# Where the first token block of layer 2 is split, and which of three prologue steps goes first, in a fused attention + two-layer kernel

## The chip, the cores and the metric

One Trainium2 chip, one of its cores. The metric is the device time of one execution in microseconds; the kernel before takes 858.0 us in the median of three runs (857.73 to 858.41).

## The reference

```
x = windowed_attention(q, k, v)                 # 4 batches, 8 heads, 576 positions, 64 per head
x = x.transpose(0, 2, 1, 3).reshape(2304, 512)
x = (sigmoid(x @ w_gate) * (x @ w_val)) @ w_out # layer 1: 512 -> 1536 -> 512
h = x @ w_in                                    # layer 2: 512 -> 2048
g = maximum(h, 0) + alpha * minimum(h, 0)
return g @ w_out2                               # 2048 -> 512
```

Heads 0 to 3 look at a plain window of 32 positions, heads 4 to 7 at a window with dilation 4. All tensors are fp32.

## The kernel before, in words

Every fp32 operand is split into two fp16 halves, high and low, and a product is three passes (high by high, high by low, low by high). ScalarE makes the high half (`activation` with a scale), VectorE or GpSimd the low one (the operand less its high half).

Layer 1 goes batch by batch, b = 0 to 3, 576 tokens each. Attention of the next batch runs between its steps, so that the last batch, b = 3, has none. For each of 12 column tiles m: the gate products (`gv_mm` "g", L584), the halves of the tile before (`gv_halves(m - 1)`: L612 on ScalarE, L170 on GpSimd in the last batch and on VectorE in the others), the sigmoid (L597, ScalarE), the value products ("v", L584), and the multiply (`gv_multiply`, L602, VectorE). The tile `gt` (the halves) feeds the output products: four chunks d of 128 columns, each a sum over the 12 tiles m (`o1_mm`, L636). A chunk leaves PSUM by L654 (ScalarE), L196 takes its bound, and L656 stores it to `y_dram`. Gate, value and output products take three pairs of PSUM banks in turn: chunk (3, 0) takes the pair that value tile 10 had, which L602 of m = 10 sets free.

Layer 2 works on token blocks: block 0 (DIRECT) holds the first 256 tokens, all of batch 0, blocks 1 to 4 hold 512 each. A block's y is read back from `y_dram` (`y_load`, L870 for block 0), sums are made on GpSimd (`y_sums`, L902 for block 0), and the high and low halves `yh` by `y_high` (L925, ScalarE) and `y_low` (L929, VectorE). The products with `w_in` are L968. Block 0 has four short units of two halves with 24 matmuls each; `last_output(d, m)`, which is called ahead of each `o1_mm` of the last batch, puts one of these eight halves into the output loop at 12 (d - 2) + m = 1, 4, 6, 9, 11, 14, 16 and 19. Blocks 1 to 4 have long units of seven products of 12 matmuls (`unit`, whose first product and its copy `c1`, L1023, are `unit_begin`). Between them stand the products with `w_out2` (L1213). What the activation leaves is split by L1050 (ScalarE) and L1054 (VectorE); the last four splits of a short unit are kept in a list and done in the next one (`sums_high`, `sums_low`).

The weights of layer 2 are prepared during layer 1 in small steps (`prepare`): sums on GpSimd (L813 to L816), high halves on ScalarE (L823), low halves on VectorE (L828), stores to `w2_dram` (L840). They come back as `w_i` (L761) and, for `w_out2`, as `plain` (a first pair of tiles, `w2_ring(True)`) and `w` (three more), L1196. SyncE's queue issues all of these DMAs in the program's order. Tiles of a few tags share slots: "sg" and "gf" (two each), "xh" (two, 4608 fp16 wide), "y" (eight). The order of all engines is the order in which the program is written.

Of the kernel before, what the change touches and what calls it, by code (L numbers as in the profile page):

```python
# [8 lines left out]
F32 = mybir.dt.float32  # L9
# [15 lines left out]
def attention_moe_kernel(  # L25
# [23 lines left out]
    P = 128  # L49
# [599 lines left out]
    def o1_y(b, d):  # L649
        i = KD * b + d  # L650
        if b == 0:
            y_scale(b, d, d + 1)
        dst = tp.tile([P, S], F32, tag="sg", name="y")
        nc.scalar.activation(halves(dst), open_.pop(("o", b, d)), AF.Copy, scale=oy[:, i:i + 1])  # L654
        bound(am_y[:, i:i + 1], dst)
        nc.sync.dma_start(out=y_dram[:, d, S * b:S * b + S], in_=dst)  # L656
# [208 lines left out]
    def y_load(j):  # L865

        t0, n = blocks[j]
        for d in range(2):
            t = y[j, d] = yp.tile([P, 2, TB], F32, tag="y", name="y")
            nc.sync.dma_start(out=t[:, :, :n], in_=y_dram[:, d::2, t0:t0 + n])  # L870

    def y_places():
        t = wp.tile([P, 8192], F16, tag="w_gv2", name="yh")
        u = [xp.tile([P, 4608], F16, tag="xh", name="yh") for _ in range(2)]
        shape = dict(d=2, i=7)
        even = [t[:, 3584 * z:3584 * z + 3584].rearrange("p (d i t) -> p d i t", **shape) for z in range(2)]
        odd = [u[z][:, :3584].rearrange("p (d i t) -> p d i t", **shape) for z in range(2)]
        yh.update({j: (even, odd)[j % 2] for j in range(NJ)})
        a = w2p.tile([P, 2, TB], F32, name="temp_w", tag="temp_w")
        free = [a[:, 0], a[:, 1], t[:, 7168:].bitcast(F32)] + [x_[:, 3584:].bitcast(F32) for x_ in u]  # L880
        temps.update(zip(("a11 0", "a12", "s1", "s2", "c1"), free))

    def y_parts(j, d):
# [12 lines left out]
    def y_sums(j, d):  # L896
        n = blocks[j][1]
        t = y[j, d]
        s = y[j, d, "sums"] = yp.tile([P, 4, TB // 2], F32, tag="y", name="ys")
        add = nc.gpsimd.tensor_tensor  # L900
        if j == DIRECT:
            add(out=s[:, 0, :n], in0=t[:, 1, :n], in1=t[:, 0, :n], op=ALU.subtract)  # L902
            return
        b11, b12, b21, b22 = (t[:, i, n // 2 * h:n // 2 * h + n // 2] for i in range(2) for h in range(2))
        add(out=s[:, 0], in0=b12, in1=b11, op=ALU.subtract)
        add(out=s[:, 1], in0=b22, in1=s[:, 0], op=ALU.subtract)
        add(out=s[:, 2], in0=b22, in1=b12, op=ALU.subtract)
        add(out=s[:, 3], in0=b21, in1=s[:, 1], op=ALU.subtract)
# [14 lines left out]
    def y_high(j, d):  # L923
        for w, src in y_parts(j, d):
            nc.scalar.activation(w[0], src, AF.Copy, scale=s_y[:, j:j + 1])  # L925
# [386 lines left out]
    with tc.manual_schedule():  # L1312
# [32 lines left out]
        def do(table, k, b):  # L1345
            if k in table and not (b == 1 and k < DONE):
                table[k]()
# [80 lines left out]

        def last_output(d, m):

            if d < 2 and m == 0:
                y_load(d)
            if (d, m) == (1, 0):
                y_places()
                short_places()
            if d == 1 and m == 2:
                y_sums(0, 0)
                y_sums(0, 1)
            if d == 1 and m in (6, 8):
                y_high(0, m // 8)  # L1440
                y_low(0, m // 8)
            if d == 2 and m == 2:
                y_sums(1, 0)
                y_sums(1, 1)
            if d == 2 and m in (6, 8):
                y_high(1, m // 8)
                y_low(1, m // 8)
            if (d, m) == (2, 0):
                i = 2 * turn["m"]
                short_order.extend([6, 7, i, i + 1])  # L1450
            if (d, m) == (2, 6):
                total_scale(0)
            if (d, m) == (3, 0):
                assert not steps, len(steps)
                w2_ring(True)
                w2_fetch(fetched.popleft())
            if d > 1 and M1 * (d - 2) + m in (1, 4, 6, 9, 11, 14, 16, 19):
                k = short_units.popleft()
                if k not in running:
                    running[k] = unit_short(DIRECT, k)  # L1460
                next(running[k])
                if not short_units or short_units[0] != k:
                    in2_release()
                    while ring_i:
                        in2_fetch(coming.popleft())


        for b in range(1, B):
            late = b == B - 1
            before, after = ({}, {}) if late else attention(b + 1)  # L1470
            if late:
                coming = deque(list(range(U)) * NJ)
                short_units = deque(n for k in range(U // 2) for n in (k, k))
                running = {}
                att.close()
                w2p = ctx.enter_context(tc.tile_pool(name="w2p", bufs=1))
            m0 = EARLY if b == 1 else 0
            for m in range(m0, M1):
                gv_mm(b, m, "g")
                if m > m0:  # L1480
                    gv_halves(b, m - 1, late)
                gv_sigmoid(b, m)
                prepare(3)
                gv_mm(b, m, "v")
                gv_multiply(b, m)
                do(before, m, b)
                do(after, m, b)
                prepare(3 - (0 if late else ATTENTION.get(m, 0)), sums=False)
                if late and m in (5, 7, 9, 11):
                    in2_fetch(coming.popleft())  # L1490
                if late and m == 3:
                    for j in range(3):
                        y_sum(j)
                    for j in range(3):
                        y_power(j)
            gv_halves(b, M1 - 1, late)
            y_scale(b, 0, KD)
            for d in range(KD):
                if d == 0 and b + 1 < B:
                    x_gate_scale(b + 1, 0, M1)  # L1500
                do(before, M1 + d, b)
                for m in range(M1):
                    if m == (6 if d == 2 else 0):
                        do(after, M1 + d, b)
                    if m in (2, 6, 10):
                        prepare(5 - (0 if late or m > 2 else ATTENTION.get(M1 + d, 0)))
                    if late:
                        last_output(d, m)
                    o1_mm(b, d, m, M1)
                o1_y(b, d)  # L1510

        assert not short_units
        sums_high()
        sums_low(4)
        second_places()
        short_order.clear()
        turn["h"] = 0
# [24 lines left out]
            slots[0] -= 1  # L1542

        w2_fetch_all()
        for j in range(1, NJ):
            slots[0] = 7 * (U // 2)
            for k in range(U // 2):
# [144 lines left out]
```

## Time and profile before

| | |
|---|---|
| runs | 858.41, 858.0, 857.73 us |
| profiled execution | 857.94 us, of which the span is 856.1 us |
| mean granted TensorE clock | 0.986 |
| PE busy | 826.2 us, 97% of the span |
| DVE, ACT, POOL busy | 601.8, 438.4, 263.8 us |
| instructions | 21080 |

PE is TensorE's matmuls, PEld its weight loads beside them, DVE is VectorE, ACT is ScalarE, POOL is GpSimd, SP is SyncE, which issues the DMAs. A group of matmuls in the timeline has its start, its duration and, in brackets, the time that the engine had stood idle before it and what ended this. Ends of matmuls are modelled, so a group is best measured from its start to the next one's.

### The profile page before, as it was taken

The page shows a single profiled execution, that of the slowest core. Times are in us where ns is not written, and L with a number is a line of the kernel's source. Part 1 is how long each engine was busy: PE and PEld are TensorE (multiplying, and loading weights), DVE is VectorE, ACT ScalarE, POOL GpSimd, SP SyncE. Part 2 cuts the span into 40 slices and gives each one's busy share as a digit, 9 for nine tenths or more (in the row PEclk, how much of TensorE's full clock was granted, in tenths as well). Part 3 has the DMA queues.
Part 4 walks back from the last instruction along what each step waited for, and adds up shares of the span by engine and source line. Part 5 has one row for each costly group of instructions (what it writes and reads, how often), then busy time and mean ns, then how long its engine had stood idle before and what let it go on. Part 6 is the DMA issues. An engine that isn't in the chain of part 4 may idle for free.

```text
span 856.1 us, 21080 instructions
## 1 busy us (share of the span) xinstructions
PE 826.2 (97%) x8994; PEld 686.5 (80%) x8994; DVE 601.8 (70%) x1046; ACT 438.4 (51%) x725; POOL 263.8 (31%) x253
## 2 busy tenths in 40 slices
PE   7699999999999999999999899998999999999998
PEld 4677787877877778777887678887888888888887
DVE  5889976776687677777859767588577577566641
ACT  4767664357435453444336556465555555454420
POOL 1324252234011011020238744343442245232220
PEclk9699999999999999999999999999999999999999
DMA  9954526334454252068667867955955655675372
GB/s 319 348 184 141 191 73 218 112 121 161 149 190 154 76 202 70 1 201 251 232 218 240 286 242 284 337 204 201 340 206 202 245 183 202 239 284 198 123 230 78
DMA packets 86621, 169.86 MB, mean 198 GB/s; under 512 B 5504, under 2 KB 57856, under 8 KB 86528
## 3 DMA queue, kind: packets, MB, share of 16 engines
q1 hardware_dynamic: 86528, 168.52, 56.8%
q8 instruction: 70, 1.15, 0.6%
q14 instruction: 23, 0.19, 0.1%
HBM read 138.72 MB, written 29.79 MB: 197 GB/s over the span
## 4 chain that ended last, share of the span: by engine, by line
PE 72%; DVE 12%; DMA 9%; ACT 3%; issue 2%; SPq 2%; POOL 0%; ACTq 0%; DVEq 0%
PE banks L584 20%; PE banks L1213 18%; PE banks L968 17%; PE banks L636 13%; DMA w_dram<-halves 2%; DVE plain L189 2%; DMA plain_dram<-plain 2%; DVE plain L185 2%; PE banks L317 2%; PE banks L431 1%; DVE halves L828 1%; DMA vc<-vk 1%; DMA q<-qbd 1%; DVE plain L181 1%; DVE gf L602 1%
## 5 line engine op out<-in xcount | busy, mean ns | idle before, releaser
L584 PE MATMUL banks<-xh,w_gv 128*128 128x288 f16 x2304 | 290.6, 287 | 0.5 <-ACT sg L597 0.3
L584 PEld LDWEIGHTS <-w_gv 128*128 128x128 f16 x2304 | 223.3, 98 | 58.4 <-issue 0.9
L968 PE MATMUL banks<-yh,w_i 128*128 128x256 f16 x1536 | 189.1, 274 | 10.0 <-ACT yh L925 2.5
L968 PEld LDWEIGHTS <-w_i 128*128 128x128 f16 x1536 | 150.6, 98 | 30.3 <-issue 8.0
L636 PE MATMUL banks<-gt,w_o 128*128 128x288 f16 x1152 | 144.5, 286 | 0.9 <-POOL gt L170 0.9
L636 PEld LDWEIGHTS <-w_o 128*128 128x128 f16 x1152 | 111.8, 98 | 28.9 <-issue 1.1
L1213 PEld LDWEIGHTS <-g_gv 128*128 128x128 f16 x780 | 76.3, 98 | 8.8
L1213 PE MATMUL banks<-w,g_gv 128*128 128x256 f16 x612 | 75.5, 273 | 0.0
L1006 ACT ACTIVATE neg<-banks 128x512 f32<-128x512 f32 x72 | 42.8, 594 | 56.9 <-DVE banks L1026 40.3
L1064 POOL TENSOR_TENSOR yh<-temp_y 128x512 f32<-128x512 f32 x16 | 26.5, 1659 | 125.6 <-DVE temp_y L1014 120.8
L166 POOL TENSOR_SCALAR sc<-sc 128x1 f32<-128x1 f32 x35 | 11.7, 334 | 173.0 <-DVE sc L162 172.9
L1213 PEld LDWEIGHTS <-g_g 128*128 128x128 f16 x564 | 55.2, 98 | 6.4
L602 DVE SCALAR_TENSOR_TENSOR gf<-banks,sg 128x576 f32<-128x576 f32 x48 | 36.0, 752 | 34.4 <-PE banks L584 25.5
L597 ACT ACTIVATE sg<-banks,sc 128x576 f32<-128x576 f32 x48 | 35.3, 734 | 39.9 <-PE banks L584 30.1
L196 ACT ACTIVATE junk<-plain 128x1024 bf16<-128x1024 f32 x32 | 33.8, 1057 | 36.0 <-DVE plain L200 18.8
L170 POOL TENSOR_TENSOR gt<-gf,gt 128x576 f16<-128x576 f32 x19 | 27.7, 1457 | 75.4 <-ACT gt L612 75.2
L612 ACT ACTIVATE gt<-gf 128x576 f16<-128x576 f32 x48 | 32.4, 677 | 33.3 <-DVE gf L602 29.4
L189 DVE SCALAR_TENSOR_TENSOR plain<-words,plain 128x512 uint32<-128x512 uint32 x64 | 47.7, 765 | 1.2
L1213 PE MATMUL banks<-w,g_g 128*128 128x256 f16 x396 | 48.3, 273 | 0.0
L1054 DVE SCALAR_TENSOR_TENSOR g_gv<-temp_w,sc,g_gv 128x256 f16<-128x256 f32 (+1 forms) x37 | 26.0, 711 | 28.4 <-ACT g_gv L1050 28.4
L1023 ACT ACTIVATE temp_y<-banks 128x512 f32<-128x512 f32 x32 | 19.0, 595 | 50.9 <-PE banks L968 50.7
L185 DVE SCALAR_TENSOR_TENSOR plain<-words,plain 128x512 uint32<-128x512 uint32 x64 | 43.8, 704 | 1.2
(178 smaller groups left out, 1212.3 us busy)
## 6 DMA issues: line engine op xcount, KB each, us to landing
w_i<-wi_dram SPq DMA_DIRECT2D x40, 896.0 KB, 6.3
w<-w_dram SPq DMA_DIRECT2D x52, 512.0 KB, 8.7
words<-w_out SPq DMA_DIRECT2D x28, 512.0 KB, 5.5
plain<-w_dram SPq DMA_DIRECT2D x18, 512.0 KB, 9.5
words<-w_in SPq DMA_DIRECT2D x16, 512.0 KB, 5.2
w_dram<-halves SPq DMA_DIRECT2D x28, 256.0 KB, 5.1
q<-qbd SPq DMA_DIRECT2D x6, 1152.0 KB, 7.6
words<-w_gate SPq DMA_DIRECT2D x12, 512.0 KB, 5.3
```

What stands on the lines that cost most here:

```text
L170: engine.tensor_tensor(out=lo, in0=src, in1=hi, op=ALU.subtract)
L185: nc.vector.scalar_tensor_tensor(out=d, in0=hi, scalar=0xC0000000, in1=d, op0=ALU.bitwise_and, op1=ALU.bitwise_or)
L189: nc.vector.scalar_tensor_tensor(out=d, in0=lo, scalar=29, in1=d, op0=ALU.logical_shift_right, op1=ALU.bitwise_or)
L196: nc.scalar.activation(junk[:, :src.shape[1]], src, AF.Square, accum_out=dst)
L584: nc.tensor.matmul(ps[:, h, :], lhsT=a, rhs=x_[:, H2 * h:H2 * h + H2], start=(kk == 0 and i == 0), stop=(kk == KD - 1 and i == 2),)
L597: nc.scalar.activation(halves(sg), ps, AF.Sigmoid, scale=sgx[b][:, m:m + 1])
L602: nc.vector.scalar_tensor_tensor(out=halves(gf), in0=ps, scalar=2.0 ** -15, in1=halves(sg), op0=ALU.mult, op1=ALU.mult)
L612: nc.scalar.activation(t[:, 0, :], gf, AF.Copy)
L636: nc.tensor.matmul(ps[:, h, :], lhsT=a, rhs=x_[:, H2 * h:H2 * h + H2], start=(m == 0 and z == 0), stop=(m == M1 - 1 and z == 2),)
L968: nc.tensor.matmul(o, lhsT=h, rhs=l, start=(new and v == 0 and q == 1), stop=(q == total_), skip_group_check=True,)
L1006: nc.scalar.activation(t[:, :2 * n], src[:, :2 * n], AF.Relu, scale=-1.0)
L1213: nc.tensor.matmul(ps[:, H4 * t:H4 * t + H4].rearrange("p (c f) -> p c f", c=2), lhsT=a, rhs=x_, start=(first and k == 0 and t == 0 and z ...
```

## The change

Five edits, no arithmetic among them:

1. Block 0's y goes into one "y" tile; its load moves from the start of the last batch's output loop to the end of m = 4 of its gate and value loop. `y_sums` moves to the end of m = 6, and `y_high` and `y_low` from (d, m) = (1, 6) and (1, 8) to the ends of m = 7 and m = 8. The halves lie in an "xh" slot that `y_first` takes ahead of time, and so do the sums; even and odd blocks change places.
2. `gv_halves` of the last tile, m = 11, stands right behind its multiply, in batches 1 to 3, with its low half on VectorE.
3. In the last batch L654 writes to a "gf" slot, not an "sg" slot.
4. The first fetch of `w_out2` moves from (3, 0) to (3, 8) of the output loop.
5. The first product of the first long unit and its copy stand ahead of the last short unit's four late splits.

```diff
@@ o1_y
-        dst = tp.tile([P, S], F32, tag="sg", name="y")
+        dst = tp.tile([P, S], F32, tag="gf" if b == B - 1 else "sg", name="y")
@@ y_load
+        if j == DIRECT:
+            t = yp.tile([P, 2, 2, n], F32, tag="y", name="y")
+            for d in range(2):
+                y[j, d] = t[:, d]
+                nc.sync.dma_start(out=t[:, d], in_=y_dram[:, d::2, t0:t0 + n])
+            return
@@
+    def y_first():
+        n = blocks[DIRECT][1]
+        t = spans[0] = xp.tile([P, 4608], F16, tag="xh", name="yh")
+        z = 6 * n
+        yh[DIRECT] = [t[:, z * i:z * i + z].rearrange("p (d i t) -> p d i t", d=2, i=3) for i in range(2)]
+        temps["s2"] = t[:, 3584:].bitcast(F32)
@@ y_places
-        u = [xp.tile([P, 4608], F16, tag="xh", name="yh") for _ in range(2)]
+        u = [spans[0], xp.tile([P, 4608], F16, tag="xh", name="yh")]
...
@@ y_sums
         if j == DIRECT:
-            add(out=s[:, 0, :n], in0=t[:, 1, :n], in1=t[:, 0, :n], op=ALU.subtract)
+            s = y[j, d, "sums"] = temps["s2"][:, n * d:n * d + n].unsqueeze(1)
+            add(out=s[:, 0], in0=t[:, 1], in1=t[:, 0], op=ALU.subtract)
             return
@@ last_output
-            if d < 2 and m == 0:
-                y_load(d)
+            if (d, m) == (1, 0):
+                y_load(1)
...
-            if d == 1 and m == 2:
-                y_sums(0, 0)
-                y_sums(0, 1)
-            if d == 1 and m in (6, 8):
-                y_high(0, m // 8)
-                y_low(0, m // 8)
...
             if (d, m) == (3, 0):
                 assert not steps, len(steps)
+            if (d, m) == (3, 8):
                 w2_ring(True)
                 w2_fetch(fetched.popleft())
@@ the loop over m, behind gv_multiply(b, m)
+                if m == M1 - 1:
+                    gv_halves(b, m, False)
...
+                if late and m == 4:
+                    y_first()
+                    y_load(DIRECT)
+                if late and m == 6:
+                    y_sums(DIRECT, 0)
+                    y_sums(DIRECT, 1)
+                if late and m in (7, 8):
+                    y_high(DIRECT, m - 7)
+                    y_low(DIRECT, m - 7)
-            gv_halves(b, M1 - 1, late)
@@ behind the output loop
-        sums_high()
-        sums_low(4)
         second_places()
...
         w2_fetch_all()
+        unit_begin(1, 0, [w_i[0], w_i[1]])
+        sums_high()
+        sums_low(4)
```

TensorE's order is the same before and after. VectorE, in the last batch, from the multiply of m = 8 to that of m = 9; before (lines are those of each program: L929 before is L946 after):

```order
L602 SCALAR_TENSOR_TENSOR gf<-banks,sg 128x576
L828 SCALAR_TENSOR_TENSOR halves<-quarter,sc,halves 128x512
L828 SCALAR_TENSOR_TENSOR halves<-plain,sc,halves 128x512 x2
L828 SCALAR_TENSOR_TENSOR halves<-quarter,sc,halves 128x512
L828 SCALAR_TENSOR_TENSOR halves<-plain,sc,halves 128x512
L602 SCALAR_TENSOR_TENSOR gf<-banks,sg 128x576
```

and after:

```order
L602 SCALAR_TENSOR_TENSOR gf<-banks,sg 128x576
L828 SCALAR_TENSOR_TENSOR halves<-quarter,sc,halves 128x512
L828 SCALAR_TENSOR_TENSOR halves<-plain,sc,halves 128x512
L946 SCALAR_TENSOR_TENSOR yh<-y,sc,yh 128x512
L946 SCALAR_TENSOR_TENSOR yh<-yh,sc 128x256
L828 SCALAR_TENSOR_TENSOR halves<-plain,sc,halves 128x512
L828 SCALAR_TENSOR_TENSOR halves<-quarter,sc,halves 128x512
L828 SCALAR_TENSOR_TENSOR halves<-plain,sc,halves 128x512
L602 SCALAR_TENSOR_TENSOR gf<-banks,sg 128x576
```

The second pair of low halves of block 0 has come into this row of weight splits; the first pair stands one tile earlier, and all four are gone from behind the row of L828, where they stood ahead of the first L1014.

ScalarE, from the last output chunk into the first long unit; before:

```order
L654 ACTIVATE y<-banks,sc 128x576
L196 ACTIVATE junk,sc<-y 128x576
L1050 ACTIVATE g_gv<-yh,sc 128x256
L1050 ACTIVATE g_gv<-temp_w,sc 128x256
L1050 ACTIVATE g_gv<-yh,sc 128x256
L1050 ACTIVATE g_gv<-temp_w,sc 128x256
L1023 ACTIVATE yh<-banks 128x512
L1023 ACTIVATE temp_y<-banks 128x512
```

and after (L1040 is L1023 of before, L1067 is L1050):

```order
L654 ACTIVATE y<-banks,sc 128x576
L196 ACTIVATE junk,sc<-y 128x576
L1040 ACTIVATE yh<-banks 128x512
L1067 ACTIVATE g_gv<-yh,sc 128x256
L1067 ACTIVATE g_gv<-temp_w,sc 128x256
L1067 ACTIVATE g_gv<-yh,sc 128x256
L1067 ACTIVATE g_gv<-temp_w,sc 128x256
L1040 ACTIVATE temp_y<-banks 128x512
```

The copy `c1` has passed the four late splits.

SyncE's queue between the stores of output chunks 2 and 3; before:

```order
L656 DMA y_dram<-y 128x576
L1196 DMA plain<-w_dram 128x2048 x2
L761 DMA w_i_6622<-wi_dram 128x3584
L761 DMA w_i_6623<-wi_dram 128x3584
L761 DMA w_i_6624<-wi_dram 128x3584
L761 DMA w_i_6625<-wi_dram 128x3584
L656 DMA y_dram<-y 128x576
L1196 DMA w_7813<-w_dram 128x2048 x6
```

and after (L1213 is L1196 of before):

```order
L656 DMA y_dram<-y 128x576
L761 DMA w_i_6626<-wi_dram 128x3584
L761 DMA w_i_6627<-wi_dram 128x3584
L761 DMA w_i_6628<-wi_dram 128x3584
L761 DMA w_i_6629<-wi_dram 128x3584
L1213 DMA plain<-w_dram 128x2048 x2
L656 DMA y_dram<-y 128x576
L1213 DMA w_7802<-w_dram 128x2048 x6
```

The two `plain` fetches have moved behind the four `w_i` fetches.

## Rows read from the trace of the kernel before

**Rows 1.** Page, part 1 (busy us, share, instructions) and the DMA totals.
```profile
PE 826.2 (97%) x8994; PEld 686.5 (80%) x8994; DVE 601.8 (70%) x1046; ACT 438.4 (51%) x725; POOL 263.8 (31%) x253
...
DMA packets 86621, 169.86 MB, mean 198 GB/s; under 512 B 5504, under 2 KB 57856, under 8 KB 86528
```

**Rows 2.** Waits of PE, whole span: us in all, count, longest.
```profile
PE banks L968 <- DMA w_i<-wi_dram: 2.3, 2, 1.4
...
PE banks L968 <- ACT temp_y L1023: 1.0, 1, 1.0
```

**Rows 3.** Timeline 470 to 500: start us, us, engine, line, instruction, [idle before <-releaser].
```profile
474.82 0.67 ACT L612 ACTIVATE gt<-gf 128x576 f16<-128x576 f32 x1
...
477.20 1.72 POOL L170 TENSOR_TENSOR gt<-gf,gt 128x576 f16<-128x576 f32 x1
...
478.97 10.21 PE L636 MATMUL banks<-gt,w_o 128*128 128x288 f16 x82 [0.87 <-POOL gt L170]
...
490.97 0.71 ACT L925 ACTIVATE yh<-y,sc 128x512 f16<-128x512 f32 x1
...
491.72 0.27 PE L968 MATMUL banks<-yh,w_i 128*128 128x256 f16 x1 [2.54 <-ACT yh L925]
...
492.56 0.49 PE L968 MATMUL banks<-yh,w_i 128*128 128x256 f16 x3 [0.57 <-DVE yh L929]
...
494.09 3.86 PE L968 MATMUL banks<-yh,w_i 128*128 128x256 f16 x20 [1.04 <-DVE yh L929]
```

**Rows 4.** Windows of 1 us: us, busy of five engines, PEclk, DMA, GB/s.
```profile
494.00:495.00 1.00, 0.91 (x5) 0.66 (x5) 0.52 (x2) 0.97 (x3) 0.20 (x1) 0.50 1.04 368
```

**Rows 5.** Chain that ended last, in order of time: start us, us.
```profile
500.16 2.62 PE banks L968 x24
```

**Rows 6.** Timeline 500 to 560.
```profile
533.03 2.78 PE L968 MATMUL banks<-yh,w_i 128*128 128x256 f16 x24
...
534.66 0.19 ACT L196 ACTIVATION_READ_ACCUMULATOR junk<-y 128x1 f32 x1
534.75 0.49 ACT L1050 ACTIVATE g_gv<-yh,sc 128x256 f16<-128x256 f32 x1
...
536.34 0.57 ACT L1023 ACTIVATE yh<-banks 128x512 f32<-128x512 f32 x1
...
536.97 2.78 PE L968 MATMUL banks<-yh,w_i 128*128 128x256 f16 x24 [1.15 <-ACT yh L1023]
...
541.25 1.15 PE L1213 MATMUL banks<-plain,g_gv 128*128 128x256 f16 x9
...
546.49 0.49 PE L1213 MATMUL banks<-w,g_gv 128*128 128x256 f16 x3
```

**Rows 7.** Timeline 405 to 470.
```profile
454.39 1.71 POOL L816 TENSOR_TENSOR plain<-quarter,plain 128x512 f32<-128x512 f32 x1
...
454.90 3.44 DVE L828 SCALAR_TENSOR_TENSOR halves<-plain,sc,halves 128x512 f16<-128x512 f32 x2
...
458.27 0.74 DVE L828 SCALAR_TENSOR_TENSOR halves<-quarter,sc,halves 128x512 f16<-128x512 f32 x1
...
467.32 0.74 DVE L602 SCALAR_TENSOR_TENSOR gf<-banks,sg 128x576 f32<-128x576 f32 x1
...
469.61 0.65 PE L636 MATMUL banks<-gt,w_o 128*128 128x288 f16 x4
```

**Rows 8.** Lines, shapes apart: busy us, mean ns, idle before.
```profile
L170 DVE TENSOR_TENSOR gt<-gf,gt 128x576 f16<-128x576 f32 x29 | 23.5, 810 | 11.1 <-ACT gt L612 10.9
```

**Rows 9.** Timeline 515 to 552, SyncE's queue.
```profile
522.14 7.73 SPq L761 DMA_DIRECT2D w_i<-wi_dram  x4
...
534.47 4.82 SPq L1196 DMA_DIRECT2D w<-w_dram  x6
```

**Rows 10.** DMA issues from 521, then 547: queue, count, KB, us to landing.
```profile
plain<-w_dram SPq DMA_DIRECT2D x2, 512.0 KB, 5.7
...
plain<-w_dram SPq DMA_DIRECT2D x2, 512.0 KB, 10.1
```

More of the change, by code (lines that the diff above doesn't have):

```diff
@@ L870, in y_load @@
             nc.sync.dma_start(out=t[:, :, :n], in_=y_dram[:, d::2, t0:t0 + n])
+    spans = {}
+    def y_first():
[4 more added lines that the diff above has]
+        temps["s2"] = t[:, 3584:].bitcast(F32)
     def y_places():
         t = wp.tile([P, 8192], F16, tag="w_gv2", name="yh")
-        u = [xp.tile([P, 4608], F16, tag="xh", name="yh") for _ in range(2)]
+        u = [spans[0], xp.tile([P, 4608], F16, tag="xh", name="yh")]
         shape = dict(d=2, i=7)
-        even = [t[:, 3584 * z:3584 * z + 3584].rearrange("p (d i t) -> p d i t", **shape) for z in range(2)]
-        odd = [u[z][:, :3584].rearrange("p (d i t) -> p d i t", **shape) for z in range(2)]
-        yh.update({j: (even, odd)[j % 2] for j in range(NJ)})
+        odd = [t[:, 3584 * z:3584 * z + 3584].rearrange("p (d i t) -> p d i t", **shape) for z in range(2)]
+        even = [u[z][:, :3584].rearrange("p (d i t) -> p d i t", **shape) for z in range(2)]
+        yh.update({j: (even, odd)[j % 2] for j in range(NJ) if j != DIRECT})
         a = w2p.tile([P, 2, TB], F32, name="temp_w", tag="temp_w")
-        free = [a[:, 0], a[:, 1], t[:, 7168:].bitcast(F32)] + [x_[:, 3584:].bitcast(F32) for x_ in u]
+        free = [a[:, 0], a[:, 1], t[:, 7168:].bitcast(F32), temps["s2"], u[1][:, 3584:].bitcast(F32)]
         temps.update(zip(("a11 0", "a12", "s1", "s2", "c1"), free))
@@ L898, in y_sums @@
         t = y[j, d]
-        s = y[j, d, "sums"] = yp.tile([P, 4, TB // 2], F32, tag="y", name="ys")
         add = nc.gpsimd.tensor_tensor
         if j == DIRECT:
-            add(out=s[:, 0, :n], in0=t[:, 1, :n], in1=t[:, 0, :n], op=ALU.subtract)
+            s = y[j, d, "sums"] = temps["s2"][:, n * d:n * d + n].unsqueeze(1)
+            add(out=s[:, 0], in0=t[:, 1], in1=t[:, 0], op=ALU.subtract)
             return
+        s = y[j, d, "sums"] = yp.tile([P, 4, TB // 2], F32, tag="y", name="ys")
         b11, b12, b21, b22 = (t[:, i, n // 2 * h:n // 2 * h + n // 2] for i in range(2) for h in range(2))
```

## The prediction, made before the changed kernel ran

> **What bounds the kernel now.** The page comes first: PE is busy for 826.2 of 856.1 us [rows 1]. So the end is set by TensorE's own work and by the few places where it stands still or runs slowly; what another engine saves counts only where it ends a wait of PE. The second view is the list of PE's waits, where the question is which of them the change touches. The third is the timeline around each of these places, with the engine that released PE beside it. The fourth is the granted clock in slices of 1 us, for what a wait costs after it has ended.
>
> Read so, the last batch has three places with a wait. At 478.97 PE had stood for 0.87 us, until GpSimd had made the low half of the last `gt` tile: L612 had ended at 475.49, but L170 began only at 477.20 and took 1.72 [rows 3]. At 489.18 (478.97 + 10.21) the output products run out and the first short unit of block 0 is due, but its `yh` is not there: ScalarE begins it at 490.97, and PE stands for 2.54, 0.57 and 1.04 us in three bites, the last two until VectorE has the low halves [rows 3]. Behind these waits the granted clock is 0.50, the lower level (1.2 of 2.4 GHz) [rows 4], and the unit's 20 remaining matmuls take 3.86 us; 24 of the same kind in the stream a few us later take 2.62 [rows 3, 5]. At 536.97 PE had stood for 1.15 us until ScalarE had copied `c1` at 536.34 to 536.91, which it did only after four late splits from 534.75 on [rows 6]. The remaining waits of this size, 2.3 us for `w_i` and 1.0 us for a copy, lie in the long units, which the change does not touch [rows 2].
>
> **The change, part by part.**
>
> *Block 0's split, moved ahead (edit 1).* Removed: 2.54 + 0.57 + 1.04 = **4.15 us** of PE's wait, since the last pair of `yh` now stands among the L828 that run from 454.90 on [rows 7], some 30 us before 489.18. With the wait goes its follower: PE does not stand still, so I expect the full clock, and the 24 matmuls take 2.62 in place of 0.27 + 0.49 + 3.86 = 4.62, which is **2.00 us** more. The bounds of the second term are 0, if the clock fell for another reason, and 2.00; I take 2.00, since the row of the half clock stands right behind the only long stop there. Added nowhere: the instructions are the same two loads, two sums, four high and four low halves. What they now lie beside is this. On SyncE's queue the two loads go past the preparation's weight loads and stores and the four first `w_i` fetches, of which nothing is due for PE before the short units; of tag "y" they take one slot early where there were four late (two loads, two sums). GpSimd has the two sums among its tile halves. ScalarE has two pairs of at most 0.71 + 0.71 us ahead of L612 of tiles 7 and 8. The critical neighbour is VectorE: the second pair stands in the row of weight splits ahead of L602 of tiles 9 and 10, and L602 of tile 10 frees the banks of chunk (3, 0). That L602 ends at 467.32 + 0.74 = 468.06, and PE needs it at 469.61: 1.55 us of slack [rows 7]. Two instructions of the form of L828 (the same read of fp32 and fp16, at most 512 wide) take 0.74 each undisturbed, 1.48 in all, and 1.72 each, 3.44 in all, in the row that lies beside GpSimd's L816 [rows 7]. So the price lies between 0 (1.48 less than 1.55) and 3.44 - 1.55 = 1.89. I take **0.2**: half of the pair is only 256 wide, which is nearer to the lower end, but 0.07 of room is none.
>
> *The last tile's halves, earlier and on VectorE (edit 2).* L170 on VectorE has a mean of 0.81 [rows 8]; begun at 475.49, behind L612, it would end at 476.30, and PE asks at 478.97 - 0.87 = 478.10 [rows 3]. So the whole **0.87 us** goes, with 1.8 us to spare. It is bounded below by 0, if L612 itself stands behind splits that wait for stores. VectorE stands idle until L612 has ended, but behind it are weight splits alone, which the queue uses more than 40 us later (below). In batches 1 and 2 the same instruction moves ahead on VectorE; PE goes on there with work of attention, so I cost it at nothing, covered by that; without this cover it would be the 0.81.
>
> *The "gf" slots for the last y (edit 3).* The first of these L654 needs tile 10's slot, and its readers are through before tile 11's, at 478.92 [rows 3], ahead of the end of chunk 0 at 489.18. Nothing, and it takes a possible wait away from the short units' L1006, which shares "sg".
>
> *`c1` ahead of the late splits (edit 5).* ScalarE comes free at 534.66 + 0.19 = 534.85; 12 of the 24 matmuls from 533.03 on make the operand of `c1`, so it is there by about 534.4. The copy ends at 534.85 + 0.57 = 535.42, and PE asks at 536.97 - 1.15 = 535.82 [rows 6]. The whole **1.15 us** goes. The splits become 0.57 later; their products are of the last short unit, ten items and more behind 541.25. Nothing.
>
> *The first `w_out2` fetch, later (edit 4).* The first two `plain` loads are now issued behind four `w_i` fetches, that is from 522.14 + 7.73 = 529.87 on [rows 9]. A `plain` pair lands 5.7 us after its issue in one place and 10.1 in another [rows 10], so at 535.6 to 540.0. PE wants it at 541.25, or, 1.15 us nearer without the `c1` wait, at 540.10 [rows 6]. The bounds are 0 and about 1 us (landing a little later than in either row, with `w_i`'s bytes ahead of it); I take 0. The six `w` loads keep their issue at 534.47 [rows 9]; with the longer landing they are there at 544.6, and PE asks at 546.49 - 1.15 = 545.34 [rows 6]. Nothing, with 0.8 us left.
>
> *The sum*, against the profiled execution's own time, 857.94 (span 856.1 and 1.84 around it; 0.06 below the median): 857.94 - 4.15 - 2.00 - 0.87 - 1.15 + 0.2 = **850.0 us**.
>
> **The rivals.**
>
> *A. The fetch comes late.* `plain` was issued ahead of `w_i` and is now behind 3.67 MB of it. If the pair lands just over 11 us after its issue, PE waits at the first L1213 for what `c1` gave: 850.0 + 1.2 = 851.2. For it: 10.1 us has been seen. Against it: the four `w_i` are spread over 7.73 us.
>
> *B. VectorE is disturbed by GpSimd.* The trace has 1.72 beside L816 against 0.74 alone [rows 7]. If the moved pair falls beside such sums, L602 of tile 10 is 1.89 late, PE stops at the start of the output products and the clock may fall as it did in rows 4: 849.8 + 1.89 = 851.7, or with another 2.00 us 853.7. The Trainium skill, "SBUF — State Buffer", section "Who interferes with whom", has the rule behind this: a VectorE instruction with two inputs in SBUF contends with a GpSimd one that reads SBUF, and the second to be issued waits for the whole of the first. The trace agrees (1.72 against 0.74); by that rule alone the term of edit 1 would be 1.89 and not 0.2, if GpSimd were always at work.
>
> *C. Given back in the long units.* If the 2.3 us for `w_i` and the 1.0 us for a copy [rows 2] hang on something that does not move along with PE, they grow by as much as they are now: 850.0 + 3.3 = 853.3. Against it: those loads are issued when PE releases a slot.
>
> *D. Slower.* The queue is shared evenly by `w_i`, `plain` and the six `w`: 4 x 896 KB + 2 x 512 KB + 6 x 512 KB = 7.87 MB, at the page's mean of 198 GB/s [rows 1] 39.7 us from 522.14 on, so 561.9 against 540.10: 21.8 us late, 871.8 us. It decides from 8.2 us on, at which all of the gain is gone, and that is below 300 GB/s for this stretch (7.87 MB in 26.2 us). Against it: the six `w` cannot ask for any of it before 534.47, and without them 4.72 MB take 23.8 us, which is 5.9 late and still 855.9. The Trainium skill, "DMA: Bandwidth & Descriptors", section "Two DMAs through the same engine are not ordered", says that within one queue of a DMA engine descriptors start in order; by that, `plain` would stand behind `w_i` and ahead of `w`, which speaks for A and against D. No row shows it.
>
> *E. The change does not do what it says.* The first short unit waits for something else, its `w_i` or a matmul behind a weight load, and only the 0.87 and 1.15 are left: 857.94 - 2.02 = 855.9, or 857 to 858 with A.
>
> **How the numbers follow.** My forecast has 0.55, A 0.15, B 0.11, C 0.08, E 0.06 and D 0.05. The time is the likeliest case's, 850.0. The range goes down to 848.5: 849.8 without the 0.2, less the 0.7 us that the three runs spread, less 0.6 for slower matmuls elsewhere behind the half clock. It goes up to 854.0, which takes in A, B with its clock, and C, and leaves out D, E and D's milder form. About 0.2% (1.7 us) is what a measurement of this kernel can tell from no change: faster means under 856.3, and the forecast, A, B, C and two thirds of E lie there, 0.92; the last of E is within, 0.04; slower is most of D, 0.04.
>
> **What would show it.** In the profile after, step by step: no wait of PE on `yh` ahead of the first short unit; its 24 matmuls in about 2.6 us, and the clock at 1.00 from 488 to 500; no wait on `gt` some 10 us before it, with the last L170 on VectorE right behind L612; no wait on `c1`, and that copy right behind L196. Against me would be: a wait of the first L636 on VectorE's L602 (B), a wait of the first L1213 on `plain` or `w` (A, D), longer waits on `w_i` or on a copy behind 560 (C), a wait of the first short unit on `w_i` or a DMA (E). The forecast is wrong if PE's waits in the last batch and the first long unit do not shrink by some 6 us, or if the time is outside the range.

## The result, and the profile after

The changed kernel takes 848.65 us in the median of four runs (848.14 to 851.03), the kernel before 857.87 in four beside it (856.91 to 858.41); the ratio is 0.9899 (0.9879 to 0.9920). Timed again, as after_again below, the two stand at 848.81 and 858.0, 0.9899 (0.9881 to 0.9918). The forecast was 850.0 in 848.5 to 854.0: a gain of 7.9 us, where 9.2 were measured. The profiled execution took 848.14 us with a span of 846.1, and a mean granted clock of 0.990.

The waits of PE's products with `w_in` in the profile after, whole span (us in all, count, longest):

```profile
PE banks L985 <- DMA w_i<-wi_dram: 1.8, 2, 1.5
...
PE banks L985 <- ACT temp_y L1040: 1.0, 1, 1.0
PE banks L985 <- DVE temp_y L1031: 0.7, 1, 0.7
PE banks L985 <- DVE banks L1043: 0.6, 1, 0.6
```

All of them lie in the long units, where [rows 2] had the first two as well; PE's other waits all lie ahead of the last batch. The waits for `yh` and the wait for `gt` [rows 3] and the wait for `c1` [rows 6] are gone. The clock at the place of [rows 4], in a window of 1 us (us, busy of five engines, PEclk, DMA, GB/s):

```profile
494.00:495.00 1.00, 1.00 (x11) 0.87 (x9) 0.00 (x0) 0.20 (x1) 1.00 (x3) 1.00 1.12 391
```

It is 1.00 in every such window from 464 to 500. Since PE's matmuls are the same ones in the same order, the two timelines can be laid side by side. PE after:

```profile
468.72 18.54 PE L636 MATMUL banks<-gt,w_o 128*128 128x288 f16 x150
487.10 2.78 PE L985 MATMUL banks<-yh,w_i 128*128 128x256 f16 x24
489.72 2.37 PE L636 MATMUL banks<-gt,w_o 128*128 128x288 f16 x18
...
524.96 5.40 PE L985 MATMUL banks<-yh,w_i 128*128 128x256 f16 x48
...
531.86 1.15 PE L1230 MATMUL banks<-plain,g_gv 128*128 128x256 f16 x9
...
582.06 0.82 PE L1230 MATMUL banks<-w,g_gv 128*128 128x256 f16 x6
...
840.79 1.47 PE L1230 MATMUL banks<-w,g_y 128*128 128x256 f16 x12
```

and the three of these places that the rows of before do not show, in the kernel before:

```profile
497.79 2.37 PE L636 MATMUL banks<-gt,w_o 128*128 128x288 f16 x18
...
592.02 0.82 PE L1213 MATMUL banks<-w,g_gv 128*128 128x256 f16 x6
...
850.83 1.47 PE L1213 MATMUL banks<-w,g_y 128*128 128x256 f16 x12
```

| place, and what lies ahead of it | before | after | moved by | of it in this piece | the sum had |
|---|---|---|---|---|---|
| chunk (3, 0) begins | 469.61 | 468.72 | -0.89 | -0.89 | nothing |
| first short unit begins | 491.72 | 487.10 | -4.62 | -3.73 | 0.87 + 2.54 |
| the output products behind it begin | 497.79 | 489.72 | -8.07 | -3.45 | 0.57 + 1.04 + 2.00 |
| first long unit begins | 533.03 | 524.96 | -8.07 | 0.00 | nothing |
| first product with `w_out2` | 541.25 | 531.86 | -9.39 | -1.32 | 1.15 |
| behind the waits for `w_i` | 592.02 | 582.06 | -9.96 | -0.57 | nothing |
| last products | 850.83 | 840.79 | -10.04 | -0.08 | nothing |

The 0.89 us ahead of the output products are not the change's gain: PE is 1.59 us ahead by 70 us, where nothing was moved and where the executions differ from each other, and 0.70 of it is lost again by 390 us. (The first 50 us run at a mean clock of 0.80 in the one trace and 0.83 in the other, and in after_again, the same kernel as after, the output products begin at 470.29.) So the change is best read from the start of chunk (3, 0) on: S, from there to the first product with `w_out2`, is 71.64 us before and 63.14 after, 8.50 less. The sum had 8.17, less 0.2 for VectorE, 7.97.

Three readings of the terms. VectorE, after:

```profile
455.70 0.74 DVE L946 SCALAR_TENSOR_TENSOR yh<-y,sc,yh 128x512 f16<-128x512 f32 x1
456.37 1.49 DVE L946 SCALAR_TENSOR_TENSOR yh<-yh,sc 128x256 f16<-128x256 f32 x1
...
467.51 0.74 DVE L602 SCALAR_TENSOR_TENSOR gf<-banks,sg 128x576 f32<-128x576 f32 x1
...
473.82 1.76 DVE L170 TENSOR_TENSOR gt<-gf,gt 128x576 f16<-128x576 f32 x1 [1.89 <-ACT gt L612]
```

The moved pair stands in the row of weight splits and takes 0.74 and 1.49 us; L602 of tile 10 ends at 468.25, 0.47 us before 468.72, and PE does not wait for it. L170 of the last tile takes 1.76 us here, not 0.81 [rows 8], and is done at 475.58 all the same before it is asked for. ScalarE's copy `c1` and SyncE's fetches:

```profile
526.52 0.19 ACT L196 ACTIVATION_READ_ACCUMULATOR junk<-y 128x1 f32 x1
526.62 0.58 ACT L1040 ACTIVATE yh<-banks 128x512 f32<-128x512 f32 x1
...
513.68 8.21 SPq L761 DMA_DIRECT2D w_i<-wi_dram  x4
521.95 0.90 SPq L1213 DMA_DIRECT2D plain<-w_dram  x2
...
plain<-w_dram SPq DMA_DIRECT2D x2, 512.0 KB, 8.7
```

The copy is right behind L196; the `plain` pair is issued behind the four `w_i` and lands 8.7 us later, at 530.7, for 531.86.

### The profile page after: what moved, and what is told of

Read it like the earlier page. It is cut to its first block, busy times and chain, and to the rows that moved or that the text cites. A ratio compares the mean times of both kernels' runs of the same rounds, so it can differ in the third digit from the quotient of the medians.

```text
span 846.1 us, 21075 instructions
## 1 busy us (share of the span) xinstructions
PE 822.4 (97%) x8994; PEld 684.8 (81%) x8994; DVE 604.8 (71%) x1047; ACT 438.5 (52%) x725; POOL 264.3 (31%) x252
## 3 DMA queue, kind: packets, MB, share of 16 engines
q8 instruction: 70, 1.15, 0.6%
## 4 chain that ended last, share of the span: by engine, by line
PE 85%; DVE 6%; DMA 5%; ACT 2%; issue 1%; SPq 1%; POOL 0%; ACTq 0%; DVEq 0%
PE banks L584 29%; PE banks L1230 18%; PE banks L985 17%; PE banks L636 17%; PE banks L317 2%; DMA w_i<-wi_dram 2%; PE banks L431 2%; DMA vc<-vk 1%; DMA q<-qbd 1%; DVE plain L185 1%; DMA second<-kt 1%; DVE plain L189 1%; DVE g_g L1071 1%; DVE plain L181 0%; PE banks L446 0%
## 5 line engine op out<-in xcount | busy, mean ns | idle before, releaser
L985 PE MATMUL banks<-yh,w_i 128*128 128x256 f16 x1536 | 187.0, 273 | 4.2 <-DMA w_i<-wi_dram 1.8
L1023 ACT ACTIVATE neg<-banks 128x512 f32<-128x512 f32 x72 | 42.7, 593 | 53.4 <-DVE banks L1043 41.5
L602 DVE SCALAR_TENSOR_TENSOR gf<-banks,sg 128x576 f32<-128x576 f32 x48 | 36.0, 752 | 35.3 <-PE banks L584 24.8
L612 ACT ACTIVATE gt<-gf 128x576 f16<-128x576 f32 x48 | 32.4, 678 | 38.6 <-DVE gf L602 34.4
L196 ACT ACTIVATE junk<-plain 128x1024 bf16<-128x1024 f32 x32 | 33.8, 1057 | 33.7 <-DVE plain L200 16.6
L170 POOL TENSOR_TENSOR gt<-gf,gt 128x576 f16<-128x576 f32 x18 | 26.0, 1444 | 74.5 <-ACT gt L612 74.3
L1040 ACT ACTIVATE temp_y<-banks 128x512 f32<-128x512 f32 x32 | 19.0, 594 | 48.8 <-PE banks L985 48.6
```

The lines of the kernel that those rows point to most:

```text
L196: nc.scalar.activation(junk[:, :src.shape[1]], src, AF.Square, accum_out=dst)
L602: nc.vector.scalar_tensor_tensor(out=halves(gf), in0=ps, scalar=2.0 ** -15, in1=halves(sg), op0=ALU.mult, op1=ALU.mult)
L612: nc.scalar.activation(t[:, 0, :], gf, AF.Copy)
L985: nc.tensor.matmul(o, lhsT=h, rhs=l, start=(new and v == 0 and q == 1), stop=(q == total_), skip_group_check=True,)
L1023: nc.scalar.activation(t[:, :2 * n], src[:, :2 * n], AF.Relu, scale=-1.0)
```

## The experiments

S is used throughout; a time in microseconds from a single run says little next to it. The kernel before, timed beside each group of runs, had medians of 857.68 to 858.98 us. Edits 1 to 5 are numbered as in the change.

| kernel | edits in it | S | time, us |
|---|---|---|---|
| before | none | 71.64 | 857.87 |
| after, after_again | 1 2 3 4 5 | 63.14, 63.14 | 848.65, 848.81 |
| y_only | 1 | 72.45 | 857.84 |
| y_gf | 1, 3 | 66.05 | 851.51 |
| gt_only | 2 | 71.48 | 857.64, one run |
| c1_only | 5 | 70.79 | 856.44, one run |
| after_sg | 1 2 4 5 | 64.79 | 852.63, one run |
| fetch_back | 1 2 3 5 | 63.14 | 852.01, one run |
| fill | none, and 40 added matmuls | 69.86 | 860.24, one run |
| tile_later | 1 2 3 4 5, the halves a tile later | 63.14 | 850.97, one run |
| fetch_later | 1 2 3 4 5, the fetch later still | 63.14 | 849.32, one run |
| wi_parts | 1 2 3 4 5, `w_i` in parts | 63.14 | 849.16 |

**y_only: block 0's split alone.** The changed kernel with edits 2 to 5 undone:

```diff
-        dst = tp.tile([P, S], F32, tag="gf" if b == B - 1 else "sg", name="y")
+        dst = tp.tile([P, S], F32, tag="sg", name="y")
-            if (d, m) == (3, 8):
-                if m == M1 - 1:
-                    gv_halves(b, m, False)
+            gv_halves(b, M1 - 1, late)
+        sums_high()
+        sums_low(4)
         second_places()
-        unit_begin(1, 0, [w_i[0], w_i[1]])
-        sums_high()
-        sums_low(4)
```

> Block 0's split moved ahead, and nothing else of the change. S is the time from PE's first matmul of output chunk (3, 0) to its first product with w_out2: 71.64 us before (469.61 to 541.25), 63.14 after (468.72 to 531.86). Theory (the terms stand by themselves): the three waits and the half clock go, 4.15 + 2.00, while the 0.87 for the last gt tile and the 1.15 for c1 stay: S = 65.4 and a time of about 851.5. Rival (the later w_out2 fetch and the gf slots carry part of the gain): a wait of a short unit on something else stays, S of 66.5 or more, 852.5 or more.

Measured: 857.84 us, a ratio of 0.9998 (0.9982 to 1.0014), and S of 72.45. The edit that was to bring 6.15 us brings nothing. The short units do run without a wait and at full clock; the time is lost later. ScalarE, SyncE's queue and PE in y_only, and a window of 1 us as above:

```profile
503.55 0.60 ACT L1023 ACTIVATE neg<-banks 128x512 f32<-128x512 f32 x1 [9.13 <-DMA y_dram<-y]
...
520.67 0.73 ACT L654 ACTIVATE y<-banks,sc 128x576 f32<-128x576 f32 x1
...
521.43 0.32 SPq L656 DMA_DIRECT2D y_dram<-y  x1
521.85 0.87 SPq L1213 DMA_DIRECT2D plain<-w_dram  x2
522.83 2.94 SPq L761 DMA_DIRECT2D w_i<-wi_dram  x4
...
531.71 1.21 PE L985 MATMUL banks<-yh,w_i 128*128 128x256 f16 x6 [3.41 <-DMA w_i<-wi_dram]
533.91 7.15 PE L985 MATMUL banks<-yh,w_i 128*128 128x256 f16 x42 [0.99 <-DMA w_i<-wi_dram]
...
536.00:537.00 1.00, 1.00 (x7) 0.72 (x5) 0.00 (x0) 0.00 (x0) 0.00 (x0) 0.50 1.03 416
```

The second relu of the short units (L1023, `neg`) waits 9.13 us until a store of y has landed. `neg` and y share the two slots of "sg"; that store is chunk 1's, which SyncE's queue issued at 497.14 behind five stores of weight halves. ScalarE's instructions come in the program's order, so chunk 2 leaves PSUM at 520.67 (512.49 after), its store is issued at 521.43, and behind it the `w_i` of the first long unit. PE comes to that unit too early: it waits 3.41 and 0.99 us, and the clock falls to 0.50: 48 matmuls, which take 5.4 us at full clock, go from 531.71 to 540.90, 0.99 of it the second wait. The wait for `gt`, 0.87 before, is 1.63 here. The kernel before has the same store, and no wait for it:

```profile
495.98 0.66 SPq L656 DMA_DIRECT2D y_dram<-y  x1
...
502.86 0.60 ACT L1006 ACTIVATE neg<-banks 128x512 f32<-128x512 f32 x1 [4.22 <-PE banks L968]
```

There the relu came at 502.86, 33.25 us behind the start of chunk (3, 0), and waited for PE alone, which was late itself. In y_only it comes 33.44 us behind that start (503.55 less 470.11): PE has become faster, but the relu comes no sooner. In the kernel before the store landed 4.3 us after its issue, at 500.3, ahead of what the relu waited for, so the late `yh` had hidden this wait; in y_only it landed 6.3 us after, at 503.4.

**y_gf: with y in gf slots.** y_only with edit 3 added:

```diff
-        dst = tp.tile([P, S], F32, tag="sg", name="y")
+        dst = tp.tile([P, S], F32, tag="gf" if b == B - 1 else "sg", name="y")
```

> The kernel before with block 0's split moved ahead, as in y_only, and the last batch's y in gf slots (edits 1 and 3). In y_only the second L1023 (the short unit's relu, tag sg) stood for 9.13 us until a store of y had landed, and all of ScalarE behind it. Theory (slots): with y out of sg that wait is gone, w_i comes in time, and S is what y_only was expected to have, 65.2 to 65.6; time about 851.5. Rival (the place of the w_out2 fetch, ahead of w_i, is what held w_i back in y_only): PE still waits 2 us or more for w_i at the end of the output products, S of 67 or more.

Measured: 851.51 us, 0.9914 (0.9891 to 0.9937); S is 66.05, close above what was expected. One line is worth 6.4 us of S. The sum without rounding, 71.64 less 6.15, is 65.49; the 0.56 over it are a wait for `w_i` of 1.40 in the place of the 1.15 for `c1`, and a wait for `gt` of 1.18 in place of 0.87:

```profile
PE banks L636 <- POOL gt L170: 1.2, 1, 1.2
...
529.31 4.76 PE L985 MATMUL banks<-yh,w_i 128*128 128x256 f16 x42 [1.40 <-DMA w_i<-wi_dram]
```

**after_sg and fetch_back: the same two edits, undone in the changed kernel.**

```diff
 after_sg
-        dst = tp.tile([P, S], F32, tag="gf" if b == B - 1 else "sg", name="y")
+        dst = tp.tile([P, S], F32, tag="sg", name="y")
 fetch_back
-            if (d, m) == (3, 8):
                 w2_ring(True)
                 w2_fetch(fetched.popleft())
```

> The changed kernel with the last batch's y back in sg slots (edit 3 undone, all else kept). Theory (slots): the relu waits for the store of y again, some 8 us, chunk 2 leaves PSUM as much later, the four w_i fetches behind its store too, and PE waits for w_i: S of 68 to 71 in place of 63.14. Rival (the place of the fetch): S of 63.1 to 64.5.

> The changed kernel with the first w_out2 fetch back ahead of the w_i fetches (edit 4 undone, all else kept). Theory (slots): w_i is issued 0.9 us later and has 1 MB ahead of it, which costs 0 to 1 us: S of 63.1 to 64.1. Rival (the place of the fetch): PE waits 2 us or more for w_i ahead of the first long unit, S of 65 or more.

Measured: S is 64.79 in after_sg, between both expectations, and 63.14 in fetch_back. In after_sg the relu does wait, for 7.33 us, and the four `w_i` are issued from 520.51 on in place of 513.68, but PE hardly waits for them (0.3 us, for a weight load); it waits 1.26 us for `c1`, which ScalarE now makes late:

```profile
502.20 0.60 ACT L1023 ACTIVATE neg<-banks 128x512 f32<-128x512 f32 x1 [7.33 <-DMA y_dram<-y]
...
531.95 2.78 PE L985 MATMUL banks<-yh,w_i 128*128 128x256 f16 x24 [1.26 <-ACT yh L1040]
```

So the slots matter with the fetch moved too, but less than expected. The place of the fetch looks like a second cover: the same late `w_i` land 5.3 to 8.7 us after their issue here, with nothing ahead of them, and 8.8 to 13.6 in y_only, behind `plain`. With the slots mended, the fetch may stand in either place (fetch_back); with the fetch moved, the slots cost 1.65 us of S; with neither, and without edits 2 and 5, the gain is gone (y_only). That the fetch is the cover is read from the landings and not shown: y_only differs from after_sg in edits 2 and 5 as well, and no kernel with edits 1, 2 and 5 alone was run. The longer time of fetch_back (852.01) comes later, below.

**gt_only and c1_only.** The kernel before with edit 2 alone, and with edit 5 alone:

```diff
 gt_only
                 gv_multiply(b, m)
+                if m == M1 - 1:
+                    gv_halves(b, m, False)
-            gv_halves(b, M1 - 1, late)
 c1_only
         assert not short_units
-        sums_high()
-        sums_low(4)
         w2_fetch_all()
+        unit_begin(1, 0, [w_i[0], w_i[1]])
+        sums_high()
+        sums_low(4)
```

> The last tile's halves moved ahead (batches 1 to 3, low half on VectorE), and nothing else. Theory (it is worth something only if block 0's split is ready): PE comes to the first short unit 0.87 us sooner, but yh is made when ScalarE has time, so the wait for it grows by as much: S stays at 71.6, and the 0.5 us that batch 2 has lost in the trace after is lost here too, some 858.3 us. Rival (the terms add up, as the sum had it): S = 70.8.

> The first product and the copy c1 of the first long unit ahead of the late splits, and nothing else. Theory: the wait of 1.15 us goes and no other takes its place, S = 70.4. Rival (the first w_out2 products or the next copy wait instead): S = 71.0 to 71.6.

Measured: S of 71.48 and 70.79. In gt_only the wait for `gt` is gone and the one for `yh` has grown from 2.54 to 3.60 us:

```profile
491.30 0.27 PE L968 MATMUL banks<-yh,w_i 128*128 128x256 f16 x1 [3.60 <-ACT yh L925]
```

So edit 2 is worth its 0.87 us only together with edit 1. The 0.5 us that batch 2 was thought to lose by it cannot be put down to it: it comes from a wait of L431 near 389 us that is there, longer or shorter, with and without the edit (0.61 before, 1.14 after, 1.09 in c1_only, none in gt_only). In c1_only the first long unit begins at 533.40, and the first product with `w_out2` is at 540.30, 6.90 us later in place of 8.22 [rows 6]. That is the 1.32 of the table above; S fell by less, because the half clock behind the wait for `yh` lasted longer in this execution (the last 20 matmuls of that half take 4.43 us, 3.86 before).

**fill: why the short unit ran at half clock.** The kernel before, with added matmuls whose result is overwritten:

```diff
                 if k not in running:
+                    if not running:
+                        for _ in range(40):
+                            nc.tensor.matmul(
+                                banks[:, short_order[0], :256], lhsT=wt["o"][:, 0, 0, :P], rhs=gt[3, 0][:, 0, :256],
+                                start=True, stop=True,
+                            )
                     running[k] = unit_short(DIRECT, k)
```

> The kernel before, with 40 added matmuls of 256 columns, on data that are there, in the place where PE waits for yh; their result is overwritten. Theory (the half clock behind the wait comes from PE standing still): PE never stands still, the granted clock is 1.00 from 485 to 500, the 40 take 4.4 us in place of the wait, the unit's 24 matmuls 2.6 to 2.8 us, and S falls by 1.8 to 69.8 although work was added. Rival (the clock falls for another reason, or the unit is slow for another reason): 24 matmuls in 4 us or more, S of 71.6 or more.

Measured: S of 69.86, and the clock is 1.00 from 486 to 500. PE, and the window of 1 us in the unit:

```profile
491.19 4.53 PE L1462 MATMUL banks<-gt,w_o 128*128 128x256 f16 x40
495.56 2.78 PE L968 MATMUL banks<-yh,w_i 128*128 128x256 f16 x24
...
496.00:497.00 1.00, 1.00 (x12) 0.90 (x10) 0.41 (x1) 0.97 (x2) 0.46 (x1) 1.00 0.99 328
```

40 matmuls that compute nothing make the stretch 1.8 us shorter, by keeping PE from standing still. The other two kernels that stop for `yh`, gt_only and c1_only, have the half clock behind it as well, and none of those that do not stop there has. The whole of fill is no faster, 860.24 us: in this execution the clock fell at two other places, behind a wait of L431 at 390 us and one for `w_i` at 592, which cost about 1.5 us each.

**tile_later: the room on VectorE.** The changed kernel with:

```diff
-                if late and m in (7, 8):
-                    y_high(DIRECT, m - 7)
-                    y_low(DIRECT, m - 7)
+                if late and m in (8, 9):
+                    y_high(DIRECT, m - 8)
+                    y_low(DIRECT, m - 8)
```

> The changed kernel with both pairs of block 0's halves one tile later (behind m = 8 and 9), so that two pairs and not one stand in VectorE's row ahead of L602 of tile 10. In the trace after that row has no idle time, a pair takes 2.23 us there (0.74 and 1.49), and L602 of tile 10 ends 0.47 us ahead of chunk (3, 0). Theory (VectorE's row sets when the banks come free): PE waits for L602 at the start of the output products, 0.7 us (a pair undisturbed, 1.2 less 0.5) to 1.8. Rival (the row has slack in it: the splits behind wait for stores anyway): no wait there.

Measured: PE waits 1.16 us, but for ScalarE and in the last value products, before the output products begin:

```profile
467.12 3.10 PE L584 MATMUL banks<-xh,w_gv 128*128 128x288 f16 x24 [1.16 <-ACT sg L597]
...
463.52 0.72 ACT L823 ACTIVATE halves<-quarter,sc 128x512 f16<-128x512 f32 x1 [3.65 <-DMA quarter<-plain_dram]
...
464.76 0.71 ACT L942 ACTIVATE yh<-y,sc 128x512 f16<-128x512 f32 x1
465.38 0.49 ACT L942 ACTIVATE yh<-yh,sc 128x256 f16<-128x256 f32 x1
...
466.35 0.72 ACT L597 ACTIVATE sg<-banks,sc 128x576 f32<-128x576 f32 x1
```

The second L942 pair stands ahead of tile 10's sigmoid, behind an L823 that waits 3.65 us for weights. VectorE's L602 of tile 10 ends at 469.67, 0.38 us ahead of the output products again. The expectation missed: the size was in its range, but the engine and the place were not the ones I named; that VectorE alone would have been late was not shown.

**fetch_later: the fetch later still.** The changed kernel without `w2_fetch(fetched.popleft())` at (3, 8), so that the pair goes behind the store of chunk 3.

> The changed kernel with the first w_out2 fetch later still: behind the store of chunk 3, with the other six. In the trace after it is issued at 521.95, lands 8.7 us later, 530.7, and is wanted at 531.86; behind the store it would be issued at some 526.4. Theory (rival A of the prediction, its price measured): with a landing of 5.7 to 10.1 us PE waits 0.2 to 4.6 us at the first product with w_out2, S of 63.4 to 67.7 and more if the clock falls. Rival (with w_i through, the pair lands faster than any seen): no wait, S of 63.1.

Measured: issued at 526.25, 4.3 us later, and PE waits 1.5 us (behind the first matmul that reads the pair, so that S as it was set does not show it):

```profile
PE banks L1230 <- DMA plain<-w_dram: 1.5, 1, 1.5
```

Landing was 5.7 us after issue, where the expectation had 5.7 to 10.1. In after_again a wait of 0.3 us stands in this place, in after none: the room in the changed kernel is about zero to one microsecond, no more.

**wi_parts: the wait that is left.** The changed kernel, whose first long block fetches each pair of `w_i` in parts:

```diff
+        for part in (slice(0, 1), slice(1, 7)) if apart else (slice(0, 7),):
+            for t, u in pair:
+                nc.sync.dma_start(out=t[:, :, part], in_=wi_dram[u][:, :, part])
...
-                while coming and ring_i:
-                    in2_fetch(coming.popleft())
+                in2_fetch_all(j == 1)
```

> The changed kernel, and in the first long block each w_i tile is fetched in two DMAs, the seventh that the next unit's first product reads ahead of the other six. In the trace after PE waits 1.8 us for w_i in that block, 4.6 us after its issue, and a whole tile lands in 5.7. Theory (the landing of a whole tile sets the wait): the waits for w_i there fall under 0.4 us and the time by 1.3 to 1.8 us against after_again. Rival (more DMAs on SyncE's queue delay the w_out2 fetches behind them): a wait on w or plain comes instead, no gain.

> The changed kernel once more, beside the others on this chip: 848.0 to 849.5 us, S of 63.1 to 63.2, no wait of PE on yh, gt or c1.

Measured: 849.16 us (0.9902, 0.9887 to 0.9918) beside 848.81 for after_again. No wait for `w_i` is left, but no time is gained:

```profile
PE banks L997 <- DVE temp_y L1043: 1.7, 2, 0.8
PE banks L997 <- ACT temp_y L1052: 1.6, 2, 1.1
PE banks L997 <- DVE banks L1055: 0.6, 1, 0.6
```

The waits for VectorE and ScalarE in the same stretch grew from 2.4 to 3.9 us, mostly by two new ones of 0.83 and 0.53. From chunk (3, 0) to the last products it is 372.22 us, 372.07 in after and 372.67 in after_again. From 560 to 590 us in the trace after, PE is busy for 25.8 us and VectorE for 25.1, so VectorE has little room there. Neither the gain that was expected nor the rival I wrote, a late `w_out2` fetch, came. No version timed here is faster than the changed kernel beyond what its own runs spread.

## Why the prediction was right, step by step

- **Block 0's split, 4.15 + 2.00.** Right in its reason: fill shows that the half clock came from PE standing still. In size 3.45 of 3.61 inside the unit, from start to start: the 2.00 set 4.62, three groups up to the modelled end of the last, against 2.62, a distance of starts; by starts alone it is 1.84 (6.07 less the waits of 1.61, less 2.62). Of this 1.52 is the slow clock (20 matmuls in 3.70 us, 2.18 in the stream), and 0.32 goes with the two stops. But "nothing" for **edit 3** was the step that failed: the text called the shared "sg" slot a possible wait and priced it at zero. In y_only, with edit 1 alone, the whole 6.15 us come back, most of it at the first long unit, and edit 3 added to it is worth 6.4 us of S (y_gf). The sum came out because the change had edit 3. The step looked at what the relu waits for in the trace of before; there the late `yh` hid that it would have to wait for a store.
- **The last tile, 0.87.** Gone, and for the reason given, but L170 on VectorE took 1.76 beside GpSimd's sums, not 0.81. The room covers it: from the 475.49 of before, 1.76 would end at 477.25, still ahead of 478.10. L612 was done at 473.79 and so 0.8 us earlier, measured from the start of chunk (3, 0), than before; two weight splits of ScalarE that stood ahead of it now stand behind it, which the sum did not count on and did not need. And the term is no term by itself (gt_only).
- **`c1`, 1.15.** Measured 1.32, also alone (c1_only). In the stream a group of 24 lasts 2.78 us by the timeline, and the next begins 2.62 us behind its start; so from start to start a stop costs 0.16 more than the wait that is listed, and this was left out. The same goes, twice, for the 0.32 that the piece ahead of the first short unit has over 0.87 + 2.54. These 0.49, less the 0.16 that block 0's term had too much, are the 0.33 by which S fell more than 8.17.
- **VectorE, 0.2.** Not paid: 0.47 us of room was left. The pair's 2.23 us lie between the two bounds, 1.48 and 3.44, and 0.68 over the 1.55 us of room. The splits around it ran differently, so that PE saw none of it.
- **The fetch, 0 of 0 to 1.** 0 in after, 0.3 in after_again. Rival A's price came with another 4.3 us of delay: 1.5. D, slower through this queue, was far off: the pair landed in 8.7 us with the `w_i` ahead of it.
- **The rest.** 9.2 against 7.9: 0.5 in S (8.50 against 7.97), some 0.65 behind it, most of it a shorter wait for `w_i`, which stood at 1.4 to 2.4 us in that place in all these traces but wi_parts, without a rule that I found. What is left is less than the executions differ among each other. One slip in the chances: the forecast, A, B, C and two thirds of E add up to 0.93, not 0.92.

## What to carry to other kernels

A wait of the main engine can hide the next one: before pricing a removed wait, move everything behind it ahead by that much and ask of every instruction there what it would then wait for, its slot of a shared tag above all, and where the DMA that frees this slot stands in its queue. Terms of a sum can be worth nothing alone (the last tile's halves, block 0's split) and full value together; the experiment that does one part alone shows it. In the three kernels here that stop for `yh` (2.2 to 3.6 us, then two shorter stops), the price was the stops and then a stretch at a clock of 0.50 behind them.

## What was not expected of the hardware

The same wait does not always bring the half clock. In fetch_back PE waits 0.97 and 1.36 us for `w_i`, to a hundredth the waits of the kernel before, where the clock stays at 1.00; here it falls (a window of 1 us, as above, and PE in fetch_back; then PE in the kernel before, where the same six matmuls take 0.83 us and not 1.46):

```profile
585.00:586.00 1.00, 1.00 (x7) 0.69 (x6) 0.24 (x1) 0.63 (x2) 0.00 (x0) 0.50 1.09 422
...
581.68 0.83 PE L985 MATMUL banks<-yh,w_i 128*128 128x256 f16 x6 [0.97 <-DMA w_i<-wi_dram]
583.87 1.46 PE L985 MATMUL banks<-yh,w_i 128*128 128x256 f16 x6 [1.36 <-DMA w_i<-wi_dram]
...
589.17 0.83 PE L968 MATMUL banks<-yh,w_i 128*128 128x256 f16 x6 [0.97 <-DMA w_i<-wi_dram]
591.35 0.83 PE L968 MATMUL banks<-yh,w_i 128*128 128x256 f16 x6 [1.36 <-DMA w_i<-wi_dram]
```

Most of the difference of fetch_back's time, 852.01 with an S of 63.14, lies here: from chunk (3, 0) to the last products it is 374.20 us, 2.1 more than after. tile_later and fill have the same slow stretch there, at the same work. What decides it is open. A timed difference of 2 us in a single run of this kernel can be that alone.

A low half on VectorE, 256 wide, took 1.49 us beside GpSimd's L170, and 0.48 us where GpSimd's began behind it (L946 in tile_later at 466.17); VectorE's L170 took 1.76 beside GpSimd's L815, against a mean of 0.81. These two of GpSimd in the trace after:

```profile
455.97 1.61 POOL L170 TENSOR_TENSOR gt<-gf,gt 128x576 f16<-128x576 f32 x1 [0.74 <-ACT gt L612]
...
473.70 1.27 POOL L815 TENSOR_TENSOR quarter<-quarter 128x512 f32<-128x512 f32 x1
```

They end at 457.58 and 474.97, and the two of VectorE, which had begun 0.40 and 0.12 us behind them, end at 457.86 and 475.58, which is 0.28 and 0.61 us later: their undisturbed times less 0.2. So what VectorE pays here is what is left of GpSimd's instruction when its own begins, some one microsecond. The Trainium skill, "SBUF — State Buffer", section "Who interferes with whom", says that a VectorE instruction with two inputs in SBUF contends with a GpSimd one that reads SBUF, that the ports which they share are an exclusive lock, and that the order of issue decides which of the two blocks; the trace agrees, in which the later one ends just behind the earlier.
